# An attention recurrence with experts behind it: early halves of a load sent at their own eviction, and a new list of the preparation around the loop

## The chip, the cores and the metric

The kernel runs on one core of a Trainium2 chip. A core has five engines, each with an instruction stream of its own: PE (TensorE, matrix products; PEld are its weight loads), DVE (VectorE), ACT (ScalarE), POOL (GpSimd) and SP (SyncE, which here only issues transfers). The metric is the time of one execution on the device in microseconds (us), and lower is better.

## The reference, cut to what matters

A recurrence runs over 768 positions for 4 batches of 8 heads with head size 40, each head with a 40x40 state; its output goes through a layer of four experts with causal attention, of which each position takes two.

```python
for t in range(S):
    y[:, :, t] = np.einsum('bhd,bhde->bhe', rt, state)
    Sa = np.einsum('bhde,bhe->bhd', state, at)
    state_decay = state * wt[:, :, None, :] - np.einsum('bhd,bhe->bhde', Sa, bt)
    state = state_decay + np.einsum('bhd,bhe->bhde', vt, kt)
...
for e in range(E):
    q, k, v = x @ wq[e], x @ wk[e], x @ wv[e]
    ...
    a = softmax(causal(scale * (q @ k.transpose(0, 2, 1))))
    ye = a @ v @ wo[e]
    ...   # added to the rows whose two highest gates hold e, times the gate's weight
```

## The kernel before

The program has two parts, one behind the other. The recurrence takes the first 347 us of the span or so, the experts the rest. The diff touches the first part only, and there each engine does its instructions in the order in which the program writes them down; nothing reorders them later.

**The loop.** The positions are cut into 24 chunks of 32. A chunk has two units of 16 pairs of batch and head, which gives 48 units and as many steps n of a loop. A step has stages, and a stage has a slot number: g (0, products of the state with the prepared rows, into GT), f of the unit before (2), u (4, GT through the inverse in TT), y of the unit before (5, output and new state), v (6), t (7) and d (8). Two slots are for preparation: slot 1 stands before f up to step 33 (list `MAIN`) and behind it from step 34 on (list `TAIL`); slot 3 stands before u.

**The preparation.** Four consecutive chunks make a window; window W is used by the steps 8W to 8W+7. Chunk i is number g = 0 to 3 of its window. `prep(i)` gives its jobs by a letter each: a and s (scans on DVE), b (a small copy on ACT), c (reciprocal on DVE), x (the scaling of AB on DVE), k or p (the product KB on DVE or on GpSimd), d and q (copies of AB into GL on ACT), m and n (16 products on PE into PSUM, two evictions on DVE), w, v and e (loads, v that of AB). For chunks from 8 on with g above 1, job n does not write into GL but into LT, the "late" half.

**The way to the inverse.** Job o (`f6`) sends rows of GL, and of LT, into Ld: for g of 0 and 1 two transfers of 16 rows, for g of 2 and 3 four transfers of 8 rows, early half and late half in turn. Job l (`f7`) sends Ld into MT, one transfer for each half of the partitions; job t brings LT into GL. All these transfers and the loads are issued by SP, in order. When MT has landed, `invert(W)` sets its diagonal with a memset (C) on GpSimd and does 60 operations there, two for each j (T); DVE then transposes the result into TT in three pieces, A, D and E. u of step 8W needs E.

**The order of the work.** Steps up to 15 take their preparation from a text, `START`: a chunk's digit with its letters, "@9.7" for "step 9, slot 7", E, X and V for loads, T for operations of the inversion (i and j ahead of it for windows 1 and 2). From window 3 on two tables repeat for each window: `SIDE` for the jobs, `INV` for the inversion. Their keys are steps relative to n0 = 8(W-1), the slots are parted by "/", and "2q" is job q of the window's chunk 2.

```python
for k, part in enumerate(line.split("/")):
    for z in part.split():
        at(n0 + r, 0 if n0 + r < 0 else k, *[P[4 * W + int(z[0])][x] for x in z[1:]])
```

Of the kernel before, what the change touches and what calls it, by code (L numbers as in the profile page):

```python
# [16 lines left out]
NW, NG, C = 6, 4, 32  # L17
# [3 lines left out]
ORD = {"t": "s0", "g": "s1", "k": "k0 k1"}  # L21
ORT = {"t": "s0", "g": "s1", "u": "k0 k1"}

START = """Z0 0abcsx 1a E5 1cs 0d W2 0pn 2a 1x 2cs E4 1p 2xbp 1bd W0 0q E6 1mn 0m 3a 0o 1q W1 2nq 3cs 2md Z1 3pbx 4a 2o W4 3m 4p 1o 3qn 4c 3o 4sx 5a 4b 5c 2l 5s 4m 3d 5x E7 6a 4n 6ck 5bpn 3l C X6 V10 T4 5m 4oq W5 6s W3 T2 5q V01 6b V00 5o W9 T2 6x X7 T2 7a 4d 7c 6m T2 g0 Y0 T2 7sp 5d T2 W6 E8 V11 T2 7x 6n 7bm T2 7no T2 6o T2 7l E9 6l T2 7q T2 B iC A P k0 8a k1 @0.0 Y1 iT2 6q iT10 F0 7d H0 @0.3 8cbp iT4 @0.4 Y3 @0.5 iT2 @0.7 8s iT2 @0.8 iT2 9a @1.0 iT6 8v iT20 F1 6d iT2 @1.3 iT6 9v iT2 @1.5 8w Y2 9b @1.8 H1 @2.4 9c av iT2 @2.5 8x 9s @2.7 F2 @2.8 8e @3.3 aa 9kw 8m @4.0 9xe ac @4.3 H2 @4.4 bv 9m @4.5 aksb @4.7 F3 ax @5.4 awm @5.7 ba H3 @6.0 bc @6.3 bsk @6.4 bx 8n 9n @6.5 8q bmb iA @7.3 9o @7.4 bw 8ld ane bn ad @7.5 ao bo @7.6 8o blt @7.7 al 9d at iD bd iE @8.4 9l be @8.7 jC @9.0 9q jT2 @9.7 jT8 bq jT2 @9.8 jT2 @10.3 aq @10.5 jT4 @11.0 jT8 @11.4 jT2 @11.6 jT2 @13.5 jT2 @13.6 jT2 @13.7 jT6 @14.0 jT2 @14.3 jA jT2 @14.5 jT2 @14.6 jT4 @14.7 jT8 jD jT2 @15.7 jE"""

SIDE = {
    -9: "//////0v/0a",
    -8: "//0c/0s",
    -7: "/1v/0b/1a 0k 0w//1b///0e",
    -6: "//1c/0x 1s//1k/1w 1e",  # L30
    -5: "/2a/2v//1x 0m/2k//2e/2c",
    -4: "//1m 2s//3a/2b 3c//3v/2x",
    -3: "//2w///3s 3w//3k/2m",
    -2: "//0n/3e 3x/3b 1n/3m 0o/1o",
    -1: "0d/0l/0q//2n 3n/1l 2o/1q 3o/2l 3l",
    0: "/2t/1d/3t",
    1: "2q",
    2: "//3d",
    3: "/2d/3q",
}  # L40

INV = {
    0: "/C",
    1: "//////T18",
    2: "T8///////T5",
    4: "///////T7/T11",
    7: "/T1 A/D////T4 T6",
    8: "/E",
}

def layouts(r, k, v, w, a, b):
# [44 lines left out]
def recurrence(tc, ctx, I, xT, CM, early, tail=None):  # L96
    nc = tc.nc
# [4 lines left out]
    V, A, T, PL = nc.vector, nc.scalar, nc.tensor, nc.gpsimd  # L102
# [21 lines left out]
    def product():  # L124
        return ps([128, 4, 2, 32])
# [28 lines left out]
    Ld = [dp.tile([128, 32, 32], F32, name=f"Ld{i}") for i in range(2)]  # L154
# [8 lines left out]
    E8 = [(EWr[0], ABr[0][:, 0:512], EKr[0]), thirds(r20), (EWr[1], flat(LS[1])[:, 0:512], EKr[1]), thirds(r21),  # L163
          (flat(SC[8]), flat(XT[1][:, 4:8]), flat(KB[8])), (flat(SC[9]), flat(XT[1][:, 0:4]), LTb), (EWr[0], ABr[2][:, 0:512], EKr[0]), (EWr[1], ABr[3][:, 0:512], EKr[1])]
# [69 lines left out]
    def prep(i):  # L234

        w, g = divmod(i, NG)
        ab, sc, kb, pc = ABr[i % 4], SC[i % 12], KB[i % NKB], PC[i % 12]
        gl = GL[w % 2]
        SUF = SUFs[i % 2]
        sv = SUF[:, 1:529].rearrange("p (n c) -> p n c", c=33)  # L240
        EW, EA, EK = E8[i] if i < 8 else own[i % 2]
        EW, EK = EW[0:104], EK[0:104]
        def f0a():
            V.tensor_tensor_scan(SUF[:, 0:528][:, ::-1], EW[:, ::-1], d1[:, ::-1], 1.0, op0=OP.mult, op1=OP.add)
        def f0b():
            A.activation(pc, sv[:, ::4, 0], AF.Copy)
        def f0c():
            V.reciprocal(sc[:, ::4, 0], sv[:, ::4, 0])
        def f1():
            z = sc.rearrange("p n c -> p (n c)")  # L250
            for b in range(0, 528, 132):
                V.tensor_tensor_scan(z[:, b + 1:b + 132], EW[:, b + 1:b + 132], d1[:, 1:132], z[:, b:b + 1], op0=OP.mult, op1=OP.add)
        aa = ab[0:104, 0:512].rearrange("p (n c) -> p n c", c=32)
        bd = ab[0:104].rearrange("p (s n c) -> p s n c", s=2, c=32)
        def f2():
            if i < 8:
                V.tensor_tensor(aa, EA[0:104].rearrange("p (n c) -> p n c", c=32), sc[:, :, 0:32], op=OP.mult)
# [288 lines left out]
    for n in range(NU + 2):  # L546
# [478 lines left out]
```

## Time and profile before

| | |
|---|---|
| median of 3 runs | 584.45 us (583.21 to 586.54) |
| the profiled execution | 581.98 us |
| its span, first to last instruction | 580.2 us |
| mean granted clock of TensorE | 0.936 of 2.4 GHz |
| busy: PE, DVE, ACT, POOL | 500.1, 421.4, 428.1, 361.7 us |

The span is what the trace covers; the execution is 1.78 us longer. Times within the trace count from the span's start. Busy shares of the whole span mix both parts, so a stage has to be read by itself: a granted clock below 1 in a window says that TensorE ran at 1.2 GHz for some of it.

### The profile page before, as it was taken

What the parts mean: (1) busy time and instruction counts of PE and PEld (TensorE: products, weight loads), DVE (VectorE), ACT (ScalarE), POOL (GpSimd) and SP (SyncE); (2) the same over time, 40 slices, a digit from 0 to 9 for tenths busy, and PEclk for the clock granted to TensorE, in tenths of its full rate; (3) what the DMA queues carried; (4) which work ended last, traced back from release to release, by engine and by line L of the source; (5) the groups of instructions that cost most, each with busy time, mean ns of one, the idle gap of its engine ahead of it and who ended that gap; (6) DMA issues with size and microseconds to landing.
All of it is one profiled execution on the core that took longest, in us unless ns stands there. A gap on an engine that the chain in (4) does not pass through costs nothing. (4 is left out here: it accounts for less than half of the span.)

```text
span 580.2 us, 20194 instructions
## 1 busy us (share of the span) xinstructions
PE 500.1 (86%) x7985; PEld 433.8 (75%) x7985; DVE 421.4 (73%) x954; ACT 428.1 (74%) x1008; POOL 361.7 (62%) x623
## 2 busy tenths in 40 slices
PE   4766798778878888897998988899999999999995
PEld 3756687657767776786777778799888779888874
DVE  8887468979978997994664656877866776666661
ACT  5984678788789889886977745777766677676773
POOL 6337399539949966985883623777662838264741
PEclk9555589999999999997999989999999999999998
DMA  7866544478757658657437726322312032111111
GB/s 217 218 137 152 135 116 121 100 182 208 183 144 190 174 110 219 142 127 191 110 89 226 193 75 181 97 55 66 107 40 67 26 108 61 51 30 51 35 36 53
DMA packets 65952, 69.96 MB, mean 121 GB/s; under 512 B 31032, under 2 KB 51768, under 8 KB 65848
## 3 DMA queue, kind: packets, MB, share of 16 engines
q1 hardware_dynamic: 65704, 68.48, 45.3%
q8 instruction: 65, 1.06, 0.8%
q14 instruction: 39, 0.32, 0.2%
q10 hardware_dynamic: 144, 0.10, 0.1%
HBM read 50.20 MB, written 11.01 MB: 106 GB/s over the span
## 5 line engine op out<-in xcount | busy, mean ns | idle before, releaser
L319 POOL TENSOR_TENSOR MT<-MT,TP 128x58 f32<-128x58 f32 (+9 forms) x164 | 94.8, 578 | 12.9
L319 POOL TENSOR_TENSOR TP<-MT 128x58 f32<-128x58 f32 (+9 forms) x164 | 94.7, 577 | 12.2
L875 POOL TENSOR_TENSOR P<-P,m 128x128 f32<-128x128 f32 (+2 forms) x96 | 88.1, 939 | 3.4
L864 ACT ACTIVATE P<-P,m 128x128 f32<-128x128 f32 (+2 forms) x96 | 63.8, 665 | 18.2 <-DVE m L862 17.1
L862 DVE CUSTOM_DVE_ANT_0 P<-sc,MK 128x128 f32<-128x128 f32 (+2 forms) x96 | 59.3, 623 | 23.6 <-PE sc L855 11.6
L421 PE MATMUL py<-R,LS 128*40 128x80 f32 x1536 | 70.6, 241 | 1.4 <-DVE R L414 1.0
L421 PEld LDWEIGHTS py<-R,LS 128*40 128x40 f32 x1536 | 59.5, 121 | 9.8 <-DVE R L414 1.3
L414 DVE TENSOR_TENSOR R<-pb,CM 64x256 f32<-64x256 f32 x96 | 40.1, 418 | 31.1 <-ACT GT L389 15.3
L855 PE MATMUL sc<-ks,qs 128*128 128x384 f32 (+4 forms) x256 | 61.2, 343 | 1.5 <-DVE m L862 1.4
L400 ACT ACTIVATE R<-pu 32x320 f32<-32x320 f32 x96 | 41.1, 428 | 17.2 <-PE pu L397 14.1
L871 POOL TENSOR_TENSOR m<-m,gg 128x2 f32<-128x2 f32 x48 | 10.3, 215 | 69.6 <-DVE m L870 53.6
L883 PE MATMUL pt<-CM,P 128*128 128x128 f32 x336 | 52.1, 275 | 1.1 <-ACT pt L889 0.4
L883 PEld LDWEIGHTS pt<-CM,P 128*128 128x128 f32 x336 | 39.8, 140 | 6.3 <-ACT pt L889 1.5
L855 PEld LDWEIGHTS sc<-ks,qs 128*128 128x128 f32 x256 | 40.2, 189 | 4.2 <-DVE m L862 3.1
L389 ACT ACTIVATE GT<-pb,OWN 128x160 f32<-128x160 f32 x96 | 32.6, 390 | 14.0 <-PE pb L387 12.9
L779 PE MATMUL pt<-xh,wq 128*128 128x384 f32 x192 | 41.1, 348 | 1.9 <-DVE pt L887 1.2
L901 PE MATMUL ot<-pt,vv 128*64 128x256 f32 (+1 forms) x384 | 41.6, 359 | 0.0
L453 ACT ACTIVATE LS<-pt 40x320 f32<-40x320 f32 x92 | 39.6, 430 | 2.2
L889 ACT ACTIVATE pt<-pt 128x512 f32<-128x512 f32 (+1 forms) x64 | 34.3, 540 | 9.3 <-PE pt L883 8.4
L406 ACT ACTIVATE VU<-pb 80x512 f32<-80x512 f32 x48 | 28.5, 593 | 16.6 <-PE pb L405 9.4
L397 PE MATMUL pu<-GT,TT 64*33 64x80 f32 x768 | 24.0, 242 | 19.1 <-ACT GT L389 11.5
L901 PEld LDWEIGHTS ot<-pt,vv 128*64 128x64 f32 x384 | 25.4, 136 | 14.5 <-issue 3.7
(163 smaller groups left out, 1222.3 us busy)
## 6 DMA issues: line engine op xcount, KB each, us to landing
EK<-in_EK SPq DMA_DIRECT2D x20, 416.0 KB
ks<-ks SPq DMA_DIRECT2D x32, 192.0 KB
R<-in_VG SPq DMA_DIRECT2D x24, 208.0 KB
EW<-in_EA SPq DMA_DIRECT2D x20, 214.5 KB
R<-in_VT SPq DMA_DIRECT2D x48, 80.0 KB
R<-in_RT SPq DMA_DIRECT2D x24, 160.0 KB
RB<-in_RB SPq DMA_DIRECT2D x48, 80.0 KB
xT<-XT SPq DMA_DIRECT2D x48, 80.0 KB
```

The lines of the kernel that those rows point to most:

```text
L319: return [lambda: e.tensor_tensor(tmp, row, col, op=OP.mult), lambda: e.tensor_tensor(o, o, tmp, op=OP.add)]
L400: A.activation(r2[32:64, 40 * h0:40 * h0 + 640].rearrange("q (z p e) -> q z p e", z=2, p=2)[:, :, x], PU[64 * x:64 * x + 32, :, 0:160], AF ...
L414: V.tensor_tensor(o[:, :, x], p_f[64 * x:64 * x + 64], mask[x][:, None, None, :].to_broadcast([64, 4, 2, 32]), op=OP.mult)
L421: T.matmul(py[64 * s:64 * s + 40, p // 4, p % 4], ls[:, h, :], m, start=True, stop=True, tile_position=(0, 64 * s))
L453: A.activation(o, i, AF.Copy)
L779: T.matmul(p, w, x, start=(j == 0), stop=(j == len(prs) - 1))
L855: T.matmul(ps[:, c, 0:cw], QS[b][:, e, o], KS[b][:, e, z, k], start=(z == 0), stop=(z == 1))
L862: V.tensor_tensor_reduce(pv, ps[:, 0:ch, 0:cw], MK[:, 768 - n:768].rearrange("p (c k) -> p c k", c=ch), 1.0, 3e38, OP.add, OP.min, m[:, 0, ...
L864: later(DE, lambda: A.activation(P[:, 0:n], P[:, 0:n], AF.Exp, bias=m[:, 0, t:t + 1], scale=-1.0, accum_out=m[:, 1, t:t + 1]))
L875: PL.tensor_tensor(P[:, 0:n], P[:, 0:n], m[:, 3, t:t + 1].to_broadcast([128, n]), op=OP.mult)
L883: T.transpose(p[:, 128 * y:128 * y + 128], st["P"][t][:, 128 * c:128 * c + 128], ident)
L901: T.matmul(po[h, 128:256] if one else po[h], VV[b][:, k, 2 * ep + s], P[:, 256 * k:256 * k + (128 if one else 256)], start=(k == 0), stop= ...
```

## The change

The rows of a late chunk go out in two jobs: h sends the early halves as soon as job m has evicted them, o then only the late halves. The two loads of AB move behind MT on SP. The three tables are written anew: `START` and `SIDE` put many jobs half a step or a step elsewhere, and `INV` puts E ahead of f and spreads the operations T over other slots. Which operations there are, their shapes and the number of transfers stay as they were. The core of the diff, with `START` and most of `SIDE` left out:

```diff
 SIDE = {
...
-    -2: "//0n/3e 3x/3b 1n/3m 0o/1o",
-    -1: "0d/0l/0q//2n 3n/1l 2o/1q 3o/2l 3l",
...
-    1: "2q",
...
+    -2: "/2h/0n/3x/3e 3b 1n/3m/1o/3h/0o 0l",
+    -1: "0q//0d//2n 3n/2o 1l/3o/1q 2l 3l",
...
 INV = {
...
-    7: "/T1 A/D////T4 T6",
-    8: "/E",
+    7: "T1/A/D////T3//T2",
+    8: "E",
...
-            late = c == 2 and i >= 8 and g > 1
+            late = c == 2 and own_half
...
-        def f6():
+        own_half = i >= 8 and g > 1
+        def f6(half=0):
             for s, b in enumerate(bs):
-                late = i >= 8 and g > 1
-                nc.sync.dma_start(Ld[w % 2][b:b + (8 if late else 16)].rearrange("n j t -> j n t"), gl[32:64, g, 0:8 if late else 16, s])
-                if late:
+                if half:
+                    nc.sync.dma_start(Ld[w % 2][b:b + 8].rearrange("n j t -> j n t"), gl[32:64, g, 0:8, s])
+                elif own_half:
                     nc.sync.dma_start(Ld[w % 2][b + 8:b + 16].rearrange("n j t -> j n t"), LT[g - 2][32:64, :, s])
+                else:
+                    nc.sync.dma_start(Ld[w % 2][b:b + 16].rearrange("n j t -> j n t"), gl[32:64, g, :, s])
...
-                    ... o=f6, l=f7, ...
+                    ... o=f6, h=lambda: f6(1), l=f7, ...
```

What stands where on three engines. First SP, late in the preparation of window 4, which is used from step 32 on. Before, up to the transfer into MT:

```order
L286 DMA Ld_136<-GLe 32x8x32
L288 DMA Ld_136<-LT 32x8x32
L286 DMA Ld_136<-GLe 32x8x32
L288 DMA Ld_136<-LT 32x8x32
L353 DMA R_128<-in_VT 32x640
L286 DMA Ld_136<-GLe 32x8x32
L288 DMA Ld_136<-LT 32x8x32
L286 DMA Ld_136<-GLe 32x8x32
L288 DMA Ld_136<-LT 32x8x32
L173 DMA AB_111<-in_EA 40x512 x2
L292 DMA MT_117<-Ld_136 64x1024 x2
```

After, from the early halves of chunk 2 (the first line below) to the load of AB:

```order
L286 DMA Ld_136<-GLe 32x8x32 x2
L290 DMA Ld_136<-GLe 32x16x32 x2
L288 DMA Ld_136<-LT 32x8x32 x2
L355 DMA R_128<-in_VT 32x640
L288 DMA Ld_136<-LT 32x8x32 x2
L294 DMA MT_117<-Ld_136 64x1024 x2
L353 DMA R_126<-in_VG 32x1664
L442 DMA xT<-XT_132 40x4x128 x4
L172 DMA AB_111<-in_EA 40x512 x2
```

Between the first late half (a transfer from LT) and the transfer into MT there stood nine transfers; now there are four, with the early halves ahead of them and AB's load behind MT.

Then ACT at the steps 24 and 25, where GT (L389, then L391) and R (L400, then L402) are the stages g and u, and LS a copy of the state or of the turned KB. Before, from v of step 24 on:

```order
L406 ACTIVATE VU_129<-pb_79 80x512
L453 ACTIVATE LS_122<-pt 40x8x40
L389 ACTIVATE GT_134<-pb_78,OWN 128x4x40 x2
L453 ACTIVATE LS_122<-pt 40x8x40
L265 ACTIVATE GLe<-AB_113 40x4x4x32
L246 ACTIVATE PC_94<-SUF_88 104x4
L400 ACTIVATE R_127<-pu 32x2x160 x2
```

After, from the same place on:

```order
L245 ACTIVATE PC_94<-SUF_88 104x4
L372 ACTIVATE LS_122<-pt 64x320
L372 ACTIVATE LS_123<-pt 64x320
L408 ACTIVATE VU_129<-pb_79 80x512
L264 ACTIVATE GLe<-AB_113 40x4x4x32
L455 ACTIVATE LS_122<-pt 40x8x40
L391 ACTIVATE GT_134<-pb_78,OWN 128x4x40 x2
L455 ACTIVATE LS_122<-pt 40x8x40
L402 ACTIVATE R_127<-pu 32x2x160 x2
```

A copy of AB into GL (L265) and one into PC (L246) stood between GT and R of step 25; now the copy of AB stands behind v of step 24, and PC's before it.

Last DVE around step 40, where the pieces of MT are transposed into TT (L321, then L323) and R<-pb is f. Before:

```order
L321 STREAM_TRANSPOSE TT_121<-MT_118 128x8x32
L321 STREAM_TRANSPOSE TT_121<-MT_118 128x16x32
L429 TENSOR_TENSOR R_125<-py,PC_94 40x8x40 x2
L435 TENSOR_TENSOR XT_132<-py,SC_98 104x8x32
L414 TENSOR_TENSOR R_128<-pb_79,CM 64x4x64 x2
L321 STREAM_TRANSPOSE TT_121<-MT_118 128x8x32
```

After:

```order
L323 STREAM_TRANSPOSE TT_121<-MT_118 128x8x32
L323 STREAM_TRANSPOSE TT_121<-MT_118 128x16x32
L431 TENSOR_TENSOR R_125<-py,PC_94 40x8x40 x2
L437 TENSOR_TENSOR XT_132<-py,SC_98 104x8x32
L323 STREAM_TRANSPOSE TT_121<-MT_118 128x8x32
L416 TENSOR_TENSOR R_128<-pb_79,CM 64x4x64 x2
```

The last piece, E, stood behind f and stands ahead of it now.

## Rows read from the trace of the kernel before

**Rows 1.** Windows: us, busy of PE, PEld, DVE, ACT, POOL, granted clock, DMA share, GB/s.

```profile
14.00:75.00 61.00, 43.42 (x820) 39.74 (x824) 43.33 (x87) 43.02 (x71) 29.39 (x50) 0.50 0.64 154
76.00:115.00 39.00, 32.98 (x994) 28.95 (x992) 32.75 (x61) 30.44 (x74) 30.54 (x45) 1.00 0.44 118
212.00:260.00 48.00, 40.70 (x928) 34.49 (x928) 42.49 (x80) 41.46 (x97) 36.51 (x59) 1.00 0.63 157
260.00:270.00 10.00, 7.31 (x114) 6.45 (x116) 3.74 (x9) 5.50 (x13) 4.02 (x14) 0.66 0.66 164
```

**Rows 2.** Line L321, the transposes of MT: who it waited for: us, times.

```profile
  POOL MT L319: 4.0, 4
```

**Rows 3.** DVE's timeline at steps 16, 24, 32 and 40: start, us, instruction [idle before].

```profile
166.19 0.63 DVE L321 STREAM_TRANSPOSE TT<-MT 128x256 f32<-128x256 f32 x1 [0.80 <-POOL MT L319]
...
213.97 0.63 DVE L321 STREAM_TRANSPOSE TT<-MT 128x256 f32<-128x256 f32 x1 [0.20 <-POOL MT L319]
...
263.15 0.63 DVE L321 STREAM_TRANSPOSE TT<-MT 128x256 f32<-128x256 f32 x1 [2.67 <-POOL MT L319]
...
305.14 0.86 DVE L414 TENSOR_TENSOR R<-pb,CM 64x256 f32<-64x256 f32 x2 [0.95 <-ACT GT L389]
306.03 0.63 DVE L321 STREAM_TRANSPOSE TT<-MT 128x256 f32<-128x256 f32 x1
```

**Rows 4.** PE's timeline, u and the next g, at steps 24 and 32.

```profile
214.75 0.48 PE L397 MATMUL pu<-GT,TT 64*33 64x80 f32 x16 [1.29 <-DVE TT L321]
...
218.26 0.78 PE L387 MATMUL pb<-R,GL 128*64 128x80 f32 x16 [0.49 <-DVE R L429]
...
263.93 0.76 PE L397 MATMUL pu<-GT,TT 64*33 64x80 f32 x16 [2.61 <-DVE TT L321]
...
269.09 1.14 PE L387 MATMUL pb<-R,GLe 128*64 128x80 f32 x14
```

**Rows 5.** POOL's timeline: C of windows 4 and 5, and window 5's last addition.

```profile
220.96 0.16 POOL L304 MEMSET MT<- 128x32 f32 x1 [7.03 <-DMA MT<-Ld]
...
268.23 0.16 POOL L304 MEMSET MT<- 128x32 f32 x1 [5.11 <-DMA MT<-Ld]
...
303.43 0.26 POOL L319 TENSOR_TENSOR MT<-MT,TP 128x30 f32<-128x30 f32 x1
```

**Rows 6.** SP's timeline, window 4: the first late half and MT.

```profile
209.95 0.33 SPq L288 DMA_DIRECT2D Ld<-LT  x1
...
215.54 1.84 SPq L292 DMA_DIRECT2D MT<-Ld  x2
```

**Rows 7.** SP's timeline, window 5: from chunk 2's first half to MT.

```profile
257.14 0.42 SPq L286 DMA_DIRECT2D Ld<-GL  x1
257.78 0.34 SPq L288 DMA_DIRECT2D Ld<-LT  x1
...
260.18 0.40 SPq L288 DMA_DIRECT2D Ld<-LT  x1
...
262.08 0.45 SPq L288 DMA_DIRECT2D Ld<-LT  x1
262.70 1.63 SPq L292 DMA_DIRECT2D MT<-Ld  x2
```

**Rows 8.** ACT's timeline in step 25.

```profile
220.30 0.63 ACT L265 ACTIVATE GLe<-AB 40x512 f32<-40x512 f32 x1
220.94 0.21 ACT L246 ACTIVATE PC<-SUF 104x4 f32<-104x4 f32 x1
```

**Rows 9.** DVE's timeline: f behind step 25's copies, 1m's eviction at step 28.

```profile
225.55 0.87 DVE L414 TENSOR_TENSOR R<-pb,CM 64x256 f32<-64x256 f32 x2 [1.25 <-PE pb L411]
...
238.28 0.86 DVE L280 TENSOR_TENSOR GL<-pb,CM 64x256 f32<-64x256 f32 x2 [0.29 <-PE pb L278]
```

**Rows 10.** DVE's timeline in the opening.

```profile
20.20 0.88 DVE L280 TENSOR_TENSOR GLe<-pb,CM 64x256 f32<-64x256 f32 x2 [0.83 <-PE pb L276]
```

**Rows 11.** DVE's timeline in step 4: the eviction of 9m.

```profile
90.37 0.86 DVE L280 TENSOR_TENSOR GLe<-pb,CM 64x256 f32<-64x256 f32 x2 [1.23 <-PE pb L278]
```

More of the change, by code (lines that the diff above doesn't have):

```diff
@@ L22 @@
 ORT = {"t": "s0", "g": "s1", "u": "k0 k1"}
-START = """Z0 0abcsx 1a E5 1cs 0d W2 0pn 2a 1x 2cs E4 1p 2xbp 1bd W0 0q E6 1mn 0m 3a 0o 1q W1 2nq 3cs 2md Z1 3pbx 4a 2o W4 3m 4p 1o 3qn 4c 3o 4sx 5a 4b 5c 2l 5s 4m 3d 5x E7 6a 4n 6ck 5bpn 3l C X6 V10 T4 5m 4oq W5 6s W3 T2 5q V01 6b V00 5o W9 T2 6x X7 T2 7a 4d 7c 6m T2 g0 Y0 T2 7sp 5d T2 W6 E8 V11 T2 7x 6n 7bm T2 7no T2 6o T2 7l E9 6l T2 7q T2 B iC A P k0 8a k1 @0.0 Y1 iT2 6q iT10 F0 7d H0 @0.3 8cbp iT4 @0.4 Y3 @0.5 iT2 @0.7 8s iT2 @0.8 iT2 9a @1.0 iT6 8v iT20 F1 6d iT2 @1.3 iT6 9v iT2 @1.5 8w Y2 9b @1.8 H1 @2.4 9c av iT2 @2.5 8x 9s @2.7 F2 @2.8 8e @3.3 aa 9kw 8m @4.0 9xe ac @4.3 H2 @4.4 bv 9m @4.5 aksb @4.7 F3 ax @5.4 awm @5.7 ba H3 @6.0 bc @6.3 bsk @6.4 bx 8n 9n @6.5 8q bmb iA @7.3 9o @7.4 bw 8ld ane bn ad @7.5 ao bo @7.6 8o blt @7.7 al 9d at iD bd iE @8.4 9l be @8.7 jC @9.0 9q jT2 @9.7 jT8 bq jT2 @9.8 jT2 @10.3 aq @10.5 jT4 @11.0 jT8 @11.4 jT2 @11.6 jT2 @13.5 jT2 @13.6 jT2 @13.7 jT6 @14.0 jT2 @14.3 jA jT2 @14.5 jT2 @14.6 jT4 @14.7 jT8 jD jT2 @15.7 jE"""
+START = """0abc Z0 0sx 1a E5 1cs 0d W2 0pn 1x 2acs 0m E4 1p 2xbp 1db W0 0q 1m E6 3a 0o W1 1n 2nq 1q 3cs 2m 3b 2d Z1 3px 4a 2o W4 3m 4p 1o 3n 4b 3q 4c 3o 4sx 5acs 3d 4m E7 5x 6ac 4n 2l 6k 5pbn 3l C X6 V10 T2 5m 4oq T2 6s W5 W3 T2 5q 6b V01 V00 5o W9 T2 6x X7 T2 7a 4d 7c 6m T2 g0 Y0 5d T2 7p T2 7s W6 E8 V11 T2 7x 6n 7bm T2 7no T2 6qo T2 7l 6l 7q T4 B A iC P k0 E9 8a iT2 k1 @0.0 iT2 Y1 iT2 F0 H0 iT2 @0.3 8c iT2 8bp 7d iT2 @0.4 Y3 @0.7 8s @0.8 iT14 9a @1.0 iT10 8v iT8 9v iT6 F1 iT2 6d iT2 @1.3 iT4 @1.5 8w Y2 @1.8 H1 @2.4 av iT2 @2.5 8x @2.6 9c @2.7 F2 @2.8 8e 9s @3.3 9b aa 8m @3.7 9kw @4.0 9e ac @4.3 H2 @4.4 9x bv 9m @4.5 akb @4.6 as @4.7 F3 ax @5.4 awmh @5.7 ba H3 @6.0 bc @6.3 bsk @6.4 bx 8n 9n @6.5 8q bmhb iA @7.3 9o aend @7.4 bw 8dl bn @7.5 ao bo @7.6 8o bt @7.7 bl alt iD bd iE @8.0 9d jC @8.4 9l be @9.0 9q jT2 @9.3 jT2 @9.7 jT6 bq @9.8 jT2 @10.5 jT4 @11.0 aq jT2 @11.4 jT10 @13.5 jT4 @13.7 jT6 @14.0 jT2 @14.3 jA jT2 @14.5 jT8 @14.6 jT2 @14.7 jT8 @15.3 jD @15.7 jE"""
@@ L26 @@
 SIDE = {
[L27 to L33, printed above, removed]
-    -2: "//0n/3e 3x/3b 1n/3m 0o/1o",
-    -1: "0d/0l/0q//2n 3n/1l 2o/1q 3o/2l 3l",
-    0: "/2t/1d/3t",
-    1: "2q",
-    2: "//3d",
-    3: "/2d/3q",
+    -9: "/////0a",
+    -8: "/0v/0c/0s/0b///0k",
+    -7: "/1v//0w////1a",
+    -6: "0e//1c 1b//0x/1k 1s/1w 1e",
+    -5: "/2a/2v//1x 0m/2k 2c//2e",
@@ L40 @@
+    -4: "////2s 3a/3v 3c 1m///2x 2b",
+    -3: "/////3s 3w/2w/3k/2m",
+    -2: "/2h/0n/3x/3e 3b 1n/3m/1o/3h/0o 0l",
+    -1: "0q//0d//2n 3n/2o 1l/3o/1q 2l 3l",
+    0: "1d//2t//3t//2q",
+    2: "/3d/////2d",
+    3: "///3q",
 }
 INV = {
[L43 to L46, printed above, removed]
-    7: "/T1 A/D////T4 T6",
-    8: "/E",
+    -1: "////////C",
+    1: "////////T31",
+    2: "T4/////T2",
+    4: "//////T12//T5",
+    7: "T1/A/D////T3//T2",
+    8: "E",
 }
@@ L297, in prep @@
         return dict(a=f0a, b=f0b, c=f0c, s=f1, x=f2, p=lambda: fk(PL), k=lambda: fk(V), d=lambda: f5(0), q=lambda: f5(1),
-                    m=lambda: mm(0), n=lambda: mm(2), o=f6, l=f7, t=f8, w=lambda: load(0), v=lambda: load(1), e=lambda: load(2))
+                    m=lambda: mm(0), n=lambda: mm(2), o=f6, h=lambda: f6(1), l=f7, t=f8, w=lambda: load(0), v=lambda: load(1), e=lambda: load(2))
     def invert(w):
```

## The prediction

> **What bounds the kernel now.** I read the windows first, since shares of the whole span mix two parts. From about 347 us on the diff touches nothing, so I carry that part over unchanged. In the recurrence no engine is full: in 212 to 260 us, six whole rounds of the loop that look alike, PE is busy 40.70 of 48.00 us, DVE 42.49, ACT 41.46, at a granted clock of 1.00 [rows 1]. The time there is a ring: g on PE, GT on ACT, f on DVE, u on PE, R on ACT, y on PE, and R again, and the preparation of later chunks is put between. What lies in front of the next ring instruction on one of these engines costs its length; what lies in a gap costs nothing.
>
> Then I asked who waits for the inversion. The transposes of MT into TT (L321) sat idle for GpSimd four times, 4.0 us in all [rows 2]. Three of them are E, the last slice: 0.80 us at step 16, 0.20 at step 24, 2.67 at step 32 [rows 3]. At step 40 E comes after f and finds its data ready: the chain's last addition ended at 303.43 + 0.26 = 303.69, E began at 306.03 [rows 3, 5].
>
> The wait at step 32 costs more than itself. PE sat 2.61 us before u(32) [rows 4], and the stretch 260 to 270 has a granted clock of 0.66 [rows 1], so the clock fell to 1.2 GHz within it. From u to the next g it takes 263.93 to 269.09, 5.16 us; eight steps earlier, at 2.4 GHz, 214.75 to 218.26, 3.51 us; and g itself 1.14 with two records missing, 1.30 in proportion for all sixteen, against 0.78 [rows 4]; I take 1.21, between the two.
>
> Last, why that chain ended late. It runs from the memset C at 220.96 for 42.2 us, and C came 7.03 us after GpSimd had nothing to do, released by the load of MT [rows 5]. The load is the last thing in SP's row: the first late half is issued at 209.95, but MT only at 215.54 to 217.38 [rows 6].
>
> **The change, part by part.** *The order on SP.* Before, all eight Ld transfers of chunks 2 and 3 of a window stand behind the last evictions, with a load of VT among them, and in window 4 two AB loads. After, four early halves have gone before, and AB stands behind MT. In window 5 six issues from 257.14 to 260.18 take 3.04 us, 0.51 each [rows 7]. From the first late half on, 2 + VT + 2 = 5 issues remain, 2.55 us, and MT then needs what it does now, from the end of the last Ld issue (262.08 + 0.45 = 262.53) to the end of its own (262.70 + 1.63 = 264.33), 1.8 us [rows 7]. Window 5: 257.78 + 2.55 + 1.8 = 262.1 instead of 264.33, **2.2 earlier**. Window 4: 209.95 + 2.55 + 1.8 = 214.3 instead of 217.38, **3.1 earlier** [rows 6]. The number of transfers and their bytes stay the same.
>
> Nearest to what MT really waits for is the second of its two issues: one issue's 0.5 before the end, 263.83, so 1.3 us for a Ld to land. The Trainium skill ("DMA: Bandwidth & Descriptors", "Anatomy of one DMA — SWDGE (gpsimd) path") gives about 2.0 us of fixed cost for each DMA, most of it the receipt of the last byte, for another way of issuing. By that figure, an estimate, MT would be 0.7 later than I have it, and the sum 6.5 instead of 7.2; the row decides.
>
> *Step 32.* The chain of window 4 ends 3.1 earlier against the steps around its start. DVE came to E at 263.15 − 2.67 = 260.48 [rows 3], and by the edits of 24 to 31 below it comes 0.85 earlier by the same measure. Of 2.67 there remain 2.67 − 3.1 + 0.85 = 0.4, so −2.3. PE's wait before u(32) shrinks with it from 2.61; at step 24 PE waited 1.29 there with E idle for 0.20, and the clock stayed at 1.00 [rows 1, 3, 4], so I take full speed: u to g −1.65 and g −0.43. **Together −4.4** (bounds: −2.3, if the clock falls all the same; −4.8, without any wait left).
>
> *Step 16.* Its window has the same order on SP; the 0.80 of E [rows 3] goes: **−0.8**. *Step 24:* **−0.2**. Bounds for both: nothing to all.
>
> *Step 40.* E now stands before f. Window 5's chain starts 2.2 earlier against its steps, the others 7.4 by then (sums below), so the chain is the bound: it ends at 303.69 − 3.0 − 2.2 = 298.5 (3.0 is what is gained before its start). E then ends at about 299.2, just 306.66 − 7.45; f comes 0.86 behind it, at 300.1, where y(39) wants it at about 299.8. **+0.2** (bounds 0 and +0.9, f's whole length).
>
> *Rounds of the loop.* 2q and 0b stood on ACT in step 25 between GT and R: 0.63 + 0.21 = 0.84 us in front of R [rows 8]; after, in gaps one step earlier. DVE's 1.25 us wait for f just behind it [rows 9] is what this delay is worth downstream. The product 1m stood on PE before u at step 28, and DVE waited 0.29 for it [rows 9]; after, it stands behind y and goes to PU, which is empty then. Both recur in each window. Of 0.84 + 0.29 I take 0.65, since the two copies still need ACT somewhere: for steps 17 to 23 **−0.65**, for 25 to 31 **−0.65** (0 to −1.1 each). For steps 9 to 15, which come from the list START and get a like order only in part, **−0.5** (0 to −1.0). 1k before 1s, 2c before d, 0k half a step earlier: one DVE instruction passes another of a gap, no ring instruction waits; nothing, as long as DVE has 5.5 us idle in 48 [rows 1].
>
> *START.* DVE waited 0.83 for PE between evictions [rows 10]; in the new list other work stands there. MT(0) goes behind all the first Ld and before E7's and E9's transfers, so the first inversion begins earlier. I take that wait alone: **−0.8** (−1.8, if the inversion's lead counts too, by a second wait as long; +1.5, a wait like that of rows 11 and what it costs behind, if E9's loads, now later, are late). *Step 4:* the scaling 9x (L259, on DVE) stood ahead of f and the product 9m; now it stands between f and 9m, so 9m starts later. DVE waits 1.23 us for that product already [rows 11], a wait that 9x now partly fills and partly moves to PE; I give half of it back: **+0.6** (0 to +1.2).
>
> **Sum:** −0.8 + 0.6 − 0.5 − 0.8 − 0.65 − 0.2 − 0.65 = −3.0 before step 32; −4.4 there; +0.2 at step 40; **−7.2**. The profiled execution took 581.98 us (span 580.2 and 1.78 around it), the median of the runs is 584.45, 2.47 above. 581.98 − 7.2 = 574.8; for the median **577.2**. A measurement of this kernel tells about 0.5%, 2.9 us, from no change.
>
> **Rivals.**
> 1. *As summed*: −5.5 to −9.5, 575 to 579, chance 0.62.
> 2. *The clock falls at step 32 all the same*: the remaining wait is long enough, because the chain's pace changes or MT comes later. Then the gain is 7.2 − 2.1 = 5.1: 579.3. For it: the fall began with one wait of 2.6 [rows 4], and I have the 0.4 only as a difference of larger numbers. Against it: 1.29 at step 24 did no harm. The Trainium skill ("TensorE: Matmul & The Clock Gate", "Part 1: The HAM clock gate") says that throttled is the default and activity lifts it; the trace agrees so far, as a PE idle for 2.61 us came first [rows 4]. Chance 0.13.
> 3. *The transfers are not what holds the chain*: the early halves only change places, the late halves still land when they did (the DMA engines are busy 63% there [rows 1]), and MT starts at 217 as now. The change then does not do what it says; only ACT's and DVE's places and START remain: 0.8 − 0.6 + 0.5 + 1.3 = 2.0, minus what the E waits take of it: 582.5, no change that can be told. Against it: SP issued without any stop between 257.14 and 260.18, so issue and not landing filled the row. Chance 0.15.
> 4. *The opening stays at half clock longer*, on the other side. From 14 to 75 us the granted clock is 0.50, 1.2 GHz, though PE is busy 43.42 of 61.00 us, and from 76 us on it is 1.00 [rows 1]. The new START reorders PE's gaps there, and a rise that comes later costs 1.65/5.16 = 0.32 us for each us of it [rows 4]. From 22 us later on (7.2/0.32) the kernel is slower than before, from 32 us on by more than can be told: above 587.4. Against it: the loop's ordering of PE after 76 us hardly changes. Chance 0.05. The remaining 0.05 is a gain above 9.5, START at its bound and both windows at theirs: about 573.
>
> **Chances and range.** Faster by over 0.5% is below 581.5: cases 1 and 2, the last 0.05, and a little of case 3, 0.82. Within 0.5%: most of case 3 and a mild case 4, 0.13. Slower: 0.05. The range 573 to 581.5 leaves out most of cases 3 and 4; the likeliest case alone is 575 to 579.
>
> **What would show it.** Right: on SP, MT issued about 4.5 us after the first late half, not 7.4; C of window 4 about 3 us earlier against step 24; E at step 32 with an idle time below 1 us, the granted clock of that stretch near 1.00, and u to g about 3.5 us; ACT without copies between GT and R in step 25; E before f at step 40 with GpSimd as its releaser. Wrong: chains longer than 42.2 us because they meet other DVE work, an E wait at step 32 above 1.5 us, step 0 later than 49.1 us, or a granted clock of 0.50 past 76 us.

## The result and the profile after

| | before | changed |
|---|---|---|
| median of 5 runs | 584.83 us (583.21 to 586.56) | 578.47 us (576.06 to 587.45) |
| ratio | | 0.9894, 95% interval 0.9848 to 0.9941 |
| again, 12 runs against 35 | 583.72 us (579.05 to 589.01) | 579.45 us (576.51 to 585.57), ratio 0.9931 (0.9898 to 0.9964) |

577.2 was predicted, with 573 to 581.5 as the range, and both medians lie in it. The gain in the medians is 6.4 us with five runs and 4.3 with twelve, of 7.2 forecast. Several terms of the sum were wrong, in both directions, and the largest was paid back eight steps later. The first profile of the changed kernel lies in an execution of 587.45 us, far above its other runs, so the rows below are from a second one (584.23 us, span 582.4); where the two differ it is said.

The windows of the changed kernel (us, busy of PE, PEld, DVE, ACT, POOL, granted clock, DMA share, GB/s), where the stretch 260 to 270 answers to the last one of [rows 1]:

```profile
86.00:93.00 7.00, 5.47 (x123) 4.71 (x126) 6.03 (x10) 3.34 (x10) 6.37 (x9) 0.76 0.42 97
136.00:145.00 9.00, 5.76 (x99) 4.97 (x99) 6.75 (x11) 4.37 (x11) 8.14 (x12) 0.81 0.82 177
230.00:240.00 10.00, 8.81 (x148) 7.75 (x148) 7.61 (x14) 7.29 (x17) 9.02 (x13) 0.66 0.79 208
260.00:270.00 10.00, 8.45 (x198) 7.19 (x197) 6.72 (x16) 9.07 (x21) 1.16 (x5) 1.00 0.70 149
305.00:313.00 8.00, 6.05 (x104) 5.19 (x102) 2.99 (x7) 4.07 (x11) 3.34 (x6) 0.79 0.61 180
```

The clock is at 1.00 where it had fallen, and PE is busier there, 8.45 against 7.31 us. But it has fallen at four places, at the steps 4, 11, 27 and 40, where it had not. For the first and the third of them [rows 1] has 1.00; for the other two, before:

```profile
115.00:164.00 49.00, 40.00 (x924) 33.97 (x920) 42.29 (x80) 40.45 (x95) 35.23 (x56) 1.00 0.74 176
306.00:309.00 3.00, 2.20 (x62) 2.00 (x62) 1.06 (x2) 1.60 (x4) 0.00 (x0) 1.00 0.84 227
```

At step 11 of the changed kernel DVE waits for a load (DVE's timeline):

```profile
137.22 1.25 DVE L243 TENSOR_TENSOR_SCAN SUF<-EW,pd 104x528 f32<-104x528 f32 x1 [2.27 <-DMA EW<-in_EA]
```

Next DVE's timeline, E at steps 24, 32 and 40 [rows 3]:

```profile
215.30 0.63 DVE L323 STREAM_TRANSPOSE TT<-MT 128x256 f32<-128x256 f32 x1 [0.20 <-POOL MT L321]
...
262.67 0.66 DVE L323 STREAM_TRANSPOSE TT<-MT 128x256 f32<-128x256 f32 x1
...
306.45 0.62 DVE L323 STREAM_TRANSPOSE TT<-MT 128x256 f32<-128x256 f32 x1 [2.42 <-POOL MT L321]
306.98 0.83 DVE L416 TENSOR_TENSOR R<-pb,CM 64x256 f32<-64x256 f32 x2
```

The 2.67 us of step 32 are gone, those of step 16 too (E has no idle time there), and 2.42 us stand at step 40, where none were. PE's timeline shows what hangs on it [rows 4]: u(32) and the next g, then u(40):

```profile
264.32 0.48 PE L399 MATMUL pu<-GT,TT 64*33 64x80 f32 x16 [0.73 <-ACT GT L391]
...
267.69 0.77 PE L389 MATMUL pb<-R,GLe 128*64 128x80 f32 x16
...
307.22 0.71 PE L399 MATMUL pu<-GT,TT 64*33 64x80 f32 x16 [1.85 <-DVE TT L323]
```

u(32) to the next g takes 3.37 us at full clock (5.16 before), and u(40) has the wait and the fall. The transfers of window 4 on SP, from the first late half to MT [rows 6], and C behind them on POOL [rows 5]:

```profile
211.29 1.37 SPq L288 DMA_DIRECT2D Ld<-LT  x2
...
214.33 1.53 SPq L294 DMA_DIRECT2D MT<-Ld  x2
```

```profile
220.53 0.16 POOL L306 MEMSET MT<- 128x32 f32 x1 [5.26 <-DMA MT<-Ld]
```

And those of window 5, which set when that chain can start [rows 7]:

```profile
256.80 2.45 SPq L362 DMA_DIRECT2D RB<-in_RB  x2
259.35 0.82 SPq L286 DMA_DIRECT2D Ld<-GL  x2
260.21 0.44 SPq L651 DMA_DIRECT2D KB<-in_WD  x1
260.70 0.96 SPq L290 DMA_DIRECT2D Ld<-GL  x2
261.70 0.53 SPq L651 DMA_DIRECT2D EK<-in_WD  x1
262.32 1.78 SPq L288 DMA_DIRECT2D Ld<-LT  x2
264.20 0.39 SPq L355 DMA_DIRECT2D R<-in_VT  x1
264.69 0.86 SPq L288 DMA_DIRECT2D Ld<-LT  x2
265.73 1.55 SPq L294 DMA_DIRECT2D MT<-Ld  x2
```

Four issues stand between the first late half and MT, as forecast. Yet that half is issued at 262.32, just as step 32 starts (262.36), while before it went out 2.30 us ahead of that start (257.78 against 260.08): loads of the experts' weights (L651) and a stretched pair of RB loads are in front of it.

To compare executions I took from each trace the start of every step (the first matmul of g). The length of a step is the difference of two starts, in us:

| kernel (profiled execution) | start of step 2 | step 4 | step 7 | step 11 | step 19 | step 24 | step 27 | step 32 | step 40 | steps 32 to 40 |
|---|---|---|---|---|---|---|---|---|---|---|
| before (581.98) | 75.78 | 6.57 | 6.14 | 6.28 | 6.11 | 6.04 | 6.11 | 9.01 | 5.85 | 49.56 |
| before, again (583.09) | 75.15 | 6.69 | 6.14 | 7.56 | 6.11 | 8.56 | 6.11 | 5.20 | 5.85 | 48.36 |
| changed (587.45) | 72.76 | 9.05 | 6.29 | 10.13 | 6.12 | 6.08 | 8.52 | 5.33 | 8.56 | 49.80 |
| changed, again (584.23) | 72.94 | 9.38 | 6.29 | 9.51 | 6.11 | 6.04 | 8.50 | 5.33 | 7.75 | 49.02 |
| halves together (577.60) | 72.42 | 8.89 | 6.29 | 6.49 | 6.11 | 6.55 | 6.12 | 5.85 | 8.75 | 49.74 |
| START alone (580.26) | 72.54 | 8.88 | 6.29 | 8.60 | 6.11 | 7.36 | 6.11 | 5.20 | 7.63 | 47.72 |
| tables alone (578.42) | 75.12 | 6.73 | 7.14 | 7.03 | 7.73 | 6.02 | 6.10 | 5.82 | 6.72 | 47.00 |
| 9x first (582.30) | 72.86 | 6.76 | 6.29 | 10.22 | 6.12 | 6.07 | 8.50 | 5.34 | 8.56 | 49.85 |
| checks late (576.11) | 72.49 | 9.25 | 6.29 | 8.81 | 6.12 | 6.06 | 6.12 | 7.36 | 4.75 | 48.28 |
| both (576.89) | 72.46 | 6.75 | 7.20 | 7.06 | 8.50 | 5.75 | 6.11 | 5.31 | 5.25 | 46.55 |
| both, spread (576.61) | 73.36 | 6.77 | 7.24 | 7.49 | 6.12 | 7.38 | 6.12 | 5.32 | 7.66 | 47.10 |
| copy back (573.78) | 72.22 | 6.76 | 9.32 | 6.49 | 6.10 | 6.03 | 6.10 | 5.82 | 6.46 | 46.49 |
| EW first (572.30) | 72.66 | 6.76 | 6.98 | 5.85 | 6.12 | 6.06 | 6.12 | 5.82 | 5.85 | 45.80 |
| transfers alone (584.53) | 75.89 | 6.57 | 7.10 | 6.61 | 6.10 | 5.74 | 6.11 | 5.20 | 8.52 | 48.16 |

A second table holds the chains: how long after its step's start C comes (window 4 after step 24, window 5 after step 32), and E's idle time for GpSimd (0 for less than 0.1).

| kernel | C of window 4 | C of window 5 | E at 24 | E at 32 | E at 40 |
|---|---|---|---|---|---|
| before / again | 8.74 / 8.29 | 8.15 / 8.74 | 0.20 / 1.53 | 2.67 / 0 | 0 / 0 |
| changed / again | 6.30 / 6.98 | 9.12 / 8.67 | 0.24 / 0.20 | 0 / 0 | 3.11 / 2.42 |
| halves together | 8.35 | 9.23 | 0.70 | 1.35 | 3.39 |
| START alone | 7.61 | 8.32 | 1.54 | 0.66 | 1.40 |
| tables alone | 7.55 | 7.74 | 0.19 | 1.32 | 2.44 |
| 9x first | 7.38 | 9.09 | 0.23 | 0 | 3.11 |
| checks late | 6.62 | 6.26 | 0.23 | 1.33 | 0 |
| both | 5.25 | 7.18 | 0 | 0.64 | 0.96 |
| both, spread | 6.47 | 6.61 | 0.22 | 0 | 1.36 |
| copy back | 6.24 | 7.08 | 0.19 | 1.32 | 1.21 |
| EW first | 6.99 | 6.39 | 0.20 | 1.32 | 0.61 |
| transfers alone | 7.07 | 7.76 | 0 | 0.65 | 1.37 |

C of window 4 comes 5.25 to 7.55 us after step 24 in the ten profiles in which job h sends that window's early halves, and 7.61 to 8.74 in the four without. So the split brings the chain forward, though the nearest two (*tables alone*, *START alone*) lie only 0.06 apart.

The executions of one kernel spread over some 9 us, so a profile tells where time went in one of them and the ratios tell what an edit is worth.

### The profile page after: what moved, and what is told of

The parts are those of the page before. It is cut to its first block, busy times and chain, and to the rows that moved or that the text cites. A ratio compares the mean times of both kernels' runs of the same rounds, so it can differ in the third digit from the quotient of the medians.

```text
span 585.7 us, 20188 instructions
## 1 busy us (share of the span) xinstructions
PE 506.3 (86%) x7985; PEld 440.5 (75%) x7985; DVE 422.9 (72%) x954; ACT 428.8 (73%) x1008; POOL 360.5 (62%) x623
## 4 chain that ended last, share of the span: by engine, by line
PE 45%; POOL 14%; DVE 9%; ACT 5%; issue 5%; DMA 5%; SPq 2%; ACTq 0%; POOLq 0%; DVEq 0%
PE ot L903 7%; PE py L423 6%; POOL TP L321 6%; POOL MT L321 6%; PE sc L857 5%; PE pt L781 5%; PE pt L885 5%; PE pt L914 4%; PE pt L800 3%; PE pb L389 2%; PE pu L399 2%; ACT GT L391 2%; DMA MT<-Ld 2%; PE pb L407 1%; DMA Ld<-LT 1%
## 5 line engine op out<-in xcount | busy, mean ns | idle before, releaser
L321 POOL TENSOR_TENSOR MT<-MT,TP 128x58 f32<-128x58 f32 (+9 forms) x164 | 94.8, 578 | 12.9
L321 POOL TENSOR_TENSOR TP<-MT 128x58 f32<-128x58 f32 (+9 forms) x164 | 93.5, 570 | 12.2
L423 PE MATMUL py<-R,LS 128*40 128x80 f32 x1536 | 74.4, 248 | 4.6 <-DVE R L416 4.1
L423 PEld LDWEIGHTS py<-R,LS 128*40 128x40 f32 x1536 | 62.6, 125 | 13.7 <-DVE R L416 5.2
L402 ACT ACTIVATE R<-pu 32x320 f32<-32x320 f32 x96 | 41.2, 429 | 14.2 <-PE pu L399 10.8
L391 ACT ACTIVATE GT<-pb,OWN 128x160 f32<-128x160 f32 x96 | 32.6, 391 | 15.2 <-PE pb L389 13.6
```

The source lines that it names most:

```text
L321: return [lambda: e.tensor_tensor(tmp, row, col, op=OP.mult), lambda: e.tensor_tensor(o, o, tmp, op=OP.add)]
L391: A.activation(gt[:, :, s], p_g[:, :, 40 * s:40 * s + 40], AF.Copy, scale=OWN[:, s:s + 1])
L402: A.activation(r2[32:64, 40 * h0:40 * h0 + 640].rearrange("q (z p e) -> q z p e", z=2, p=2)[:, :, x], PU[64 * x:64 * x + 32, :, 0:160], AF ...
L423: T.matmul(py[64 * s:64 * s + 40, p // 4, p % 4], ls[:, h, :], m, start=True, stop=True, tile_position=(0, 64 * s))
```

## The experiments

My theory: MT, sent earlier, removes the wait and the fall at step 32. The rival: the new places on ACT and DVE made the gain. The first four ran together.

**The changed kernel again** (no edit).

> The changed kernel, unaltered, for more executions and another profile. First theory (the load of MT, sent earlier, took away the wait of E at step 32 and the clock's fall there): ratio 0.985 to 0.993; E at step 32 idle for under 0.5 us, u(32) to g(33) near 3.5 us at a granted clock of 1.00; and E at step 40 idle for 1 to 3 us, since the transfers of window 5 meet other loads on SP. Rival theory (the places on ACT and DVE gave the time): the same ratio, but then step 32 begins about 5 us earlier than before, against 2 to 3 by the first.

Ratio 0.9931, the upper end of what the theory had; step 32 without a wait, 5.33 us, and the wait at step 40 within what was expected (3.11 in the first profile). When step 32 begins came out as neither had it: 2.3 us later than in the execution of before (262.36 against 260.08), with falls at steps 4, 11 and 27 on the way. So the test that was to part the two theories did not.

**Halves together.** Job h is dropped, o sends all four transfers.

```diff
-                if half:
-                    nc.sync.dma_start(Ld[w % 2][b:b + 8]..., gl[32:64, g, 0:8, s])
-                elif own_half:
-                    nc.sync.dma_start(Ld[w % 2][b + 8:b + 16]..., LT[g - 2][32:64, :, s])
+                late = i >= 8 and g > 1
+                nc.sync.dma_start(Ld[w % 2][b:b + (8 if late else 16)]..., gl[32:64, g, 0:8 if late else 16, s])
+                if late:
+                    nc.sync.dma_start(Ld[w % 2][b + 8:b + 16]..., LT[g - 2][32:64, :, s])
```

> The change with the split of the transfers undone: no job h, o sends early and late halves in turn as before, all else new, AB's load still behind MT. First theory: four more issues of 0.51 us stand behind the last evictions, so MT comes 2.0 us later and E waits about 2 us at step 32: 579.5 without a fall of the clock, 581.5 with one, ratio to the kernel before 0.991 to 0.996. Rival theory: as the change, 0.989.

582.40 us, ratio 0.9979 (0.9943 to 1.0015), 2.95 above the changed kernel's median of 579.45. C of window 4 comes at 8.35, 1.4 to 2.1 later than in the two profiles of the change, and E waits at all three steps: 0.70, 1.35 and 3.39. The 2.95 is what the theory gave the split, and without it the new lists are not told from the kernel before. But the interval overlaps that of the change (0.9898 to 0.9964), and the profiled execution, 577.60 us, is shorter than both of the change. So the earlier chain is shown; what it is worth in time is likely, not shown, and the rival is not excluded.

**START alone.** Only the text `START` of the change, in the kernel before, without h.

> The kernel before with the new START alone (without job h; tables and transfers old). First theory: the first steps come 0.5 to 1.5 us earlier and step 32 still waits with the clock falling: ratio 0.996 to 0.999. Rival theory (most of the gain is made in the opening): 0.990.

0.9991 (0.996 to 1.0022), as the theory had it, but not by its reason: step 2 starts 3.24 earlier (72.54), step 4 costs 2.3 more, and E's wait lies at step 24.

**Tables alone.** The change with START of before.

> The change with the old START (window 2 then sends its halves in turn as before, windows 3 to 5 as in the change). First theory: all but the opening's gain, ratio 0.989 to 0.993, step 0 at 49.1 us and E at step 32 without a wait. Rival theory: 0.998 or more.

0.9975 (0.9935 to 1.0015): less than the theory's 0.989 to 0.993, and E did wait at step 32, 1.32 us. C of window 4 came at 7.55. START and the tables do little alone; I can't say from one profile each why they do more together.

**The kernel before again**, for a second profile. This and the next three went together.

> The kernel before, unaltered, for a second profile. First theory (E's wait at step 32 belongs to the kernel): E idle for 2 to 3 us at step 32, the granted clock below 1.00 behind it, u(32) to g(33) about 5 us. Rival theory (that wait was an accident of one execution): E idle for under 1 us there and no fall.

Neither. The wait and the fall were there, but at step 24: windows of this profile, and DVE's row for E.

```profile
212.00:222.00 10.00, 6.96 (x128) 5.92 (x123) 6.68 (x15) 5.65 (x13) 3.97 (x13) 0.83 0.67 163
260.00:270.00 10.00, 8.73 (x196) 7.44 (x193) 6.94 (x16) 8.71 (x21) 2.96 (x9) 1.00 0.54 119
```

```profile
216.51 0.63 DVE L321 STREAM_TRANSPOSE TT<-MT 128x256 f32<-128x256 f32 x1 [1.53 <-POOL MT L319]
```

With 1.53 us waited at step 24 the steps came 2.5 us later (8.56 for 6.04), and window 4's chain, already under way on SP, was ready at step 32: no wait, 5.20 us. In these two profiles the kernel before pays such a wait once, at the one step or the other.

**9x first.** In START, 9x goes back ahead of f.

```diff
-@4.0 9e ac @4.3 H2 @4.4 9x bv 9m
+@4.0 9xe ac @4.3 H2 @4.4 bv 9m
```

> The change with the scaling 9x put back ahead of f in step 4, all else as changed. In four profiles with the new START step 4 took 8.9 to 9.4 us, against 6.6 to 6.7 with the old one, and the clock fell at 88 us. First theory (9x ahead of 9m makes PE wait, and that wait brings the fall): step 4 takes 6.5 to 7 us, the clock stays at 1.00 there, the time falls by 1.5 to 2.7 us, ratio 0.986 to 0.990. Rival theory (another part of the new opening brings it): step 4 stays at 9, ratio 0.993.

Step 4 takes 6.76 us and the clock stays at 1.00 (windows of this kernel):

```profile
83.00:92.00 9.00, 7.84 (x288) 6.92 (x283) 7.58 (x14) 7.54 (x20) 8.29 (x10) 1.00 0.61 165
```

In the changed kernel PE waits for 9x, ahead of 9m (L277), behind a wait for ACT (PE's timeline):

```profile
86.48 0.48 PE L399 MATMUL pu<-GT,TT 64*33 64x80 f32 x16 [0.57 <-ACT TT L341]
88.01 0.69 PE L277 MATMUL pb<-AB,KB 104*64 104x64 f32 x16 [1.05 <-DVE AB L258]
```

So the place of 9x makes the loss at step 4, 2.3 and 2.6 us with the fall. In the ratio it does not show: 0.9919 (0.9883 to 0.9954), 579.86 us, against 0.9931 for the change, where the theory had 0.986 to 0.990. The table has a part of the reason. With the new START step 7 takes 6.29 us in all five profiles with 9x behind f, but 6.98 to 9.32 in four of the five with 9x ahead, so that step 8 starts at 113.4 us on the average of those five, against 113.8.

**Checks late.** Two blocks of the experts' weights are loaded, and checked, five steps later.

```diff
-        check_block(nc, I, stage[i][:, 0:768], i, FL, (66, 68, 60, 62)[i], jobs, 3, (6, 8, 6, 6)[i])
+        check_block(nc, I, stage[i][:, 0:768], i, FL, (66, 68, 70, 72)[i], jobs, 3, (6, 8, 6, 6)[i])
```

> The change with the four loads of experts' weights that lay on SP in steps 30 to 32 (blocks 2 and 3 of a check) five steps later, so that window 5's MT doesn't stand behind three of them. First theory (chain 5 is the bound at step 40 since its MT isn't earlier): C of window 5 comes 7 to 8 us after step 32 starts instead of 8.7 to 9.1, E waits 1 to 2 us less at step 40, steps 32 to 41 take 47 to 48 us instead of 49.0 to 49.8, ratio 0.988 to 0.991. Rival theory (MT waits for landing, not for the issues ahead of it): C at 8.5 to 9 as now, ratio 0.993.

C of window 5 comes at 6.26 instead of 9.12 and 8.67, E does not wait at step 40, and that step takes 4.75 us. The theory holds on this; SP's order, not the landing, had kept MT back. But steps 32 to 40 took 48.28, since E waited 1.33 at step 32 with a fall, and steps 38 and 39 took 5.98 and 5.79, two checks on DVE at a time. 581.93 us, 0.9946 (0.9911 to 0.9981): no gain in the whole.

**Both edits.**

> Both edits: 9x ahead of f in step 4, and the two blocks' loads later. First theory: the sum of the two, 3 to 5 us below the change, ratio 0.981 to 0.986. Rival theory: no more than the better one alone.

579.28 us, 0.9927 (0.9882 to 0.9972): the rival, no more than the better one alone. The profile has steps 32 to 40 at 46.55, but steps 38 and 39 at 5.70 and 5.82, and falls at steps 7 and 19.

**Both, spread.** The checks' operations on DVE are parted, one for each half step. (The expectations here and of *copy back* number a step by the g that ends it: "39 and 40" are 38 and 39 of the table, "20 or 28" are 19 or 27.)

```diff
-(66, 68, 70, 72)[i], jobs, 3, (6, 8, 6, 6)[i])
+(66, 68, 70, 72)[i], jobs, 3, (6, 7, 6, 7)[i])
```

> As both edits together, with the two blocks' checks spread so that no two of their DVE instructions fall on one half step: steps 39 and 40 took 5.7 to 6.0 and 5.8 us there, against 4.75 and 5.0 in the change. First theory (the ring in the tail has about 1.46 us of room a step, and two checks at once overfill it): steps 36 to 40 take 4.8 to 5.1 us each, E waits at step 40 for 0.5 to 2.5 us, since chain 5 doesn't move; steps 32 to 41 take 45.5 to 47 us, ratio 0.983 to 0.990. Rival theory (chain 5 alone sets the end): steps 32 to 41 as before this edit, 46.5 to 48.

576.13 us, ratio 0.9860 (0.9811 to 0.9908), 6 runs: the lowest ratio of all. Steps 38 and 39 take 4.73 and 5.00, E waits 1.36 at step 40, as expected, and steps 32 to 40 take 47.10, just beyond the upper end of the theory's 45.5 to 47. Its interval lies below that of the changed kernel's second measurement but for 0.001, and overlaps that of the first: faster than before, not surely faster than the change.

**Copy back.** Job 2d moves from slot 6 behind GT.

```diff
-    2: "/3d/////2d",
-    3: "///3q",
+    2: "/3d",
+    3: "/2d//3q",
```

> The same with the copy 2d (L264 on ACT) put back from slot 6 of its step, where it stands ahead of the next GT, to the next step behind GT. In four of eight profiles with the new tables step 20 or 28 took 8.5 us and the clock fell, in none with the old ones. First theory (GT comes 0.4 us later behind that copy and PE's wait for it before u, 0.99 us, starts the fall): no fall and 6.1 us at steps 20 and 28; steps 18 and 26 0.7 us longer than with the copy ahead. Rival theory (the product 1m, gone from ahead of u(20) and u(28), leaves the gap): falls as often as now.

No fall at steps 19 and 27 in its profile (6.10), but there was none in the kernel that it was made from either (6.12), so this does not tell the two theories apart. Steps 17 and 25 keep 4.89 and 4.92, so the 0.7 was wrong. (The profiles with the new tables were seven by then, not eight.) 578.03 us, 0.9893 (0.9838 to 0.9948), is not told from the kernel without the edit.

**EW first.** The load of EW goes out a step earlier.

```diff
-    -8: "/0v/0c/0s/0b///0k",
-    -7: "/1v//0w////1a",
+    -8: "/0v/0c/0s/0b 0w///0k",
+    -7: "/1v//////1a",
```

> As e9 with the load 0w of EW (a step ahead, before AB's load 1v on SP). DVE waited 1.7 to 2.3 us for EW in step 11 in most profiles with the new list, with falls of the clock behind it, and the step took 7.0 to 10.2 us. First theory (SP is late by the transfers ahead of EW): no wait for EW in step 11, which takes 5.5 to 6.5 us; 1 to 3 us less than e9 where e9 falls there. Rival theory (EW waits for a landing in front of it, not for SP's order): the wait remains above 1 us.

The scan that reads EW starts on DVE without a wait in step 11, and the step takes 5.85 us. The theory holds there; the time, 578.04 us, 0.9896 (0.9838 to 0.9954), is not told from the kernel without it.

**Transfers alone.** The kernel before with h and with AB's loads behind MT; all other places old, E behind f.

```diff
-    -9: "//////0v/0a",
-    -8: "//0c/0s",
+    -9: "///////0a",
+    -8: "/0v/0c/0s",
...
-    -2: "//0n/3e 3x/3b 1n/3m 0o/1o",
+    -2: "/2h/0n/3e 3x/3b 1n/3m 0o/1o 3h",
```

> The transfers alone: the kernel before with job h and the AB loads behind MT (START, SIDE and INV otherwise old, E behind f). First theory as it stands now (the steps are paced by the chains, and window 5's MT can't be earlier as long as weights' loads stand ahead of it): C of window 4 comes 6 to 7.3 us after step 24 starts instead of 8.3 to 8.7, E waits under 1 us at steps 24 and 32, so neither of them brings a fall; at step 40 a wait of 1 to 3 us appears instead, steps 32 to 41 take 48 to 50 us; ratio 0.993 to 0.999. Rival theory (the transfers made the whole gain): ratio 0.987 to 0.992.

As expected: C of window 4 at 7.07, no wait at step 24, 0.65 at step 32, neither with a fall; and at step 40 the wait, with step 40 at 8.52 us. DVE's timeline there:

```profile
304.13 0.85 DVE L417 TENSOR_TENSOR R<-pb,CM 64x256 f32<-64x256 f32 x2 [0.96 <-ACT GT L392]
306.36 0.62 DVE L324 STREAM_TRANSPOSE TT<-MT 128x256 f32<-128x256 f32 x1 [1.37 <-POOL MT L322]
```

E is behind f here and the step is as long as in the changed kernel (8.56, 7.75), so the new place of E is not what costs at step 40. 581.63 us, 0.9961 (0.9920 to 1.0002): not told from the kernel before, and the rival's 0.987 to 0.992 meets only the end of the interval. So START, the tables and the transfers, each alone, are not told from no change; the whole gain is measured only for all of them together.

## Why the prediction was right, point by point

The time came out in the range, and the wait and the fall at step 32 went as described. That the sum came out near is in part luck, since the errors of its terms offset each other. Neither profile of the changed kernel shows the gain as a whole: step 41 starts 2.3 and 1.7 us later than in the first profile of before, where 7.2 earlier was forecast, and the part behind it, for which nothing was forecast, took 3.1 and 0.5 longer. The gain stands in the medians, and where it lies in a usual execution is not shown.

The differences below are from the profiles: changed (both) less before (the first).

- **The bound.** Right in kind: E's wait and the fall behind it were worth 3.68 us at step 32 (9.01 to 5.33), of 4.4 forecast. But I took the step for the cause. The second profile of before shows the same loss at step 24 instead.
- **The order on SP.** Window 4's C came 2.4 and 1.8 us earlier against step 24 (2.0 and 1.3 against the second profile of before), not 3.1. The issues went as counted: from the first late half to the end of MT's issue 4.57 us, of 4.35 forecast. From the end of MT's issue to C it took 217.38 to 220.96, 3.6 us, before, and 215.86 to 220.53, 4.7 us, in the second profile: a part of the lead went in landing. From the end of the last Ld issue to MT's second it took 264.69 + 0.86 = 265.55 to 266.81, again 1.3 us. The 2.0 us that the Trainium skill gives for another way of issuing ("DMA: Bandwidth & Descriptors", "Anatomy of one DMA — SWDGE (gpsimd) path") are not borne out here, where SP issues.
- **Step 40, +0.2. This is the term that was mis-sized:** +2.7 and +1.9, beyond the bound of +0.9. I had window 5's chain 2.2 us earlier against step 32; it came 1.0 and 0.5 later (0.4 later and 0.1 earlier against the second profile of before). I had not counted what stands ahead of its halves on SP: two loads of weights, 0.97 us, and the stretched issues of RB. *Checks late* shows it: with those loads moved, SP takes 3.55 us from the start of RB's issues to the first late half instead of 5.52, C comes at 6.26, and E does not wait. Only 0.97 of these 2 us are the loads; the rest is that less is stretched. Together steps 32 to 40 gave +0.2 and −0.5, where −4.2 stood in the sum.
- **START, −0.8.** Step 0 came 0.94 and 1.05 earlier. By step 2 it was 3.02 and 2.84, which no term had. Step 1 alone took 2.1 us less. PE no longer stands still within a group of matmuls there (1.25 us, below), and the clock rises earlier; that these two make the 2.1 is argued, not shown.
- **Step 4, +0.6.** +2.5 and +2.8, beyond the bound of +1.2. The mechanism was as described, but PE's wait brought a fall, which I had priced at step 32 alone.
- **Steps 16 and the rounds.** Steps 16 to 23 gave −2.1 in both (48.06 to 46.00 and 45.97), against −0.8 and −0.65. Steps 24 to 31 took 1.0 longer, but 1.4 less without the 2.4 of step 27's fall; forecast were −0.85.
- **Step 11** was in no term: +3.9 and +3.2. DVE waits for the load of EW there, and the clock falls. The steps 8 to 15 together gave +3.8 and +3.7, where −0.5 was forecast for 9 to 15.
- **The sum.** The second profile has a time of 584.23, longer than that of before. Its falls at steps 11 and 27 cost 3.2 and 2.4; without them it would be 578.6, near the median of 579.45. That the usual execution lacks them is argued from other profiles with the same lists (step 11 at 6.49 in *halves together*, step 27 at 6.12 in *checks late*), not shown for this kernel; against it, step 11 took 8.60 us or more in five of the ten profiles with the new START.
- **The rivals.** That the clock falls all the same at step 32 did not come true; it fell at step 40 instead. That the transfers change nothing is refuted for the chain, since C of window 4 comes earlier in every profile with the split; for the time *halves together* makes it unlikely, no more. A longer opening at half clock did not occur: the clock rose earlier (granted 1.00 from 72 to 76 us in both profiles, 0.57 in that of before).

## What to carry to other kernels

In this kernel a wait for a chain that runs ahead gave the next chain slack, and taking it away moved the wait to the next chain, unless that one started earlier too. So before a wait is counted as a gain, follow the chain behind it, with every transfer in its queue, those of other parts of the program among them.

Price each new wait of TensorE with the fall of the clock that may follow, wherever it stands, and take a second profile before one execution's stall is taken as the kernel's.

## What the runs showed of the hardware

The clock fell to half after shorter waits than I had thought: behind 0.99 us before u at step 27, with the granted clock at 0.66 over the next stretch (PE's timeline of the changed kernel):

```profile
230.82 0.69 PE L413 MATMUL pb<-RB,VU 128*64 128x64 f32 x16
232.49 0.76 PE L399 MATMUL pu<-GT,TT 64*33 64x80 f32 x16 [0.99 <-ACT GT L391]
```

A longer wait, 1.29 us, passed without a fall at step 24 of before [rows 4]. In five profiles E waits 1.32 to 1.35 us at step 32; in one of them, *checks late*, the clock falls and the step takes 7.36 us, in the other four it does not, and the step takes 5.82 to 5.85. So the length of a wait alone does not tell, and the places of the falls differ between executions of one kernel. The Trainium skill ("TensorE: Matmul & The Clock Gate", "Part 1: The HAM clock gate") says that throttled is the default and activity lifts it; a PE wait stands ahead of each of the four falls above (1.05, 2.81, 0.99 and 1.85 us), which agrees.

PE can stand with nothing to wait for. In all four profiles with the old START it stopped in step 1 within a group of 64 small matmuls, for 0.67 to 1.66 us. The one of before:

```profile
66.52 0.94 PE L330 MATMUL pu<-TT,TT 16*32 16x16 f32 x54
68.71 0.39 PE L330 MATMUL pu<-TT,TT 16*32 16x16 f32 x10 [1.25 <-issue]
```

In all ten with the new START the group runs through; in the changed kernel:

```profile
65.75 1.05 PE L332 MATMUL pu<-TT,TT 16*32 16x16 f32 x64
```

What PE lacked there is not in the profile and stays open. So does what stretched the two issues of RB on SP to 2.45 us. The kernel before has such issues too: one of 1.36 us at 255.26 and one of 1.42 at 260.62, among others of 0.34 to 0.47.
